# Routing a second mixture of experts: gate products in banks of their own, gathered rows' transposes spread between matmuls, and the first row list read between the halves of its weights

## The chip, the cores and the metric

The kernel runs on one core of a Trainium2 chip. The metric is the device time of one execution in microseconds (us); lower is better. A core has five engines with a queue each: TensorE (PE in the profile: matmuls and transposes; PEld is its weight load), VectorE (DVE), ScalarE (ACT), GpSimd (POOL: here small adds, and gathers and scatters by a list of rows), and SyncE (SP: here it only issues transfers). Each engine takes its instructions in the order of its queue and waits for the other engines by semaphores.

## The reference, cut to what matters

The program is an attention layer, then a mixture of eight experts in which each token goes through all of them, then a second mixture in which each token goes through two of eight experts only. The change touches the second mixture:

```python
logits = x @ w_gate                                   # x: 1152 x 512, 8 experts
noise_scale = np.log1p(np.exp(x @ w_noise))
noisy_logits = logits + noise_scale * noise
top2 = np.argpartition(-noisy_logits, 2, axis=1)[:, :2]
top2_l = np.take_along_axis(noisy_logits, top2, axis=1)
top2_w = softmax(top2_l)                              # shortened
for e in range(8):
    for k in range(2):
        mask = top2[:, k] == e
        h = np.maximum(x[mask] @ w1[e], 0.0)          # w1: 512 x 1024
        out[mask] += top2_w[mask, k, None] * (h @ w2[e])   # w2: 1024 x 512
```

## The kernel before, in words

**Tiles.** The 1152 tokens are nine tiles of 128. `acc` holds the output of the first mixture, nine tiles of 128 x 512. All products are of float32 operands split into a high and a low part (`xh`, `xl`; `wh`, `wl`; `hh`, `hl`), so one product is three matmuls (`mm3`, L161). ACT makes the high part and DVE the low one (`split`, L98), for weights too (`conv_w`, L113). PSUM has eight banks, in four tags "a" to "d" of two banks each (`ps`, L73); a new tile of a tag waits until the tile before the last one in it has been read.

**Order.** From L893 on the order on PE, DVE and ACT is the order of the code (`manual_schedule`, L893); POOL and SP, and after L987 all engines, are put in order by a scheduler that estimates times. `mm3` takes one step from the list `between` after each matmul, so small work can be laid between the large matmuls.

**Routing.** The last expert of the first mixture is worked off in two halves of its hidden size (`g1`, `g2` with `a0`, `b0`, `a1`, `b1`), and the routing of the second runs between, for three tiles at a time (`Route`, L367: `r0` for tiles 0 to 2, `r3`, `r6`). `turn` writes a tile of `acc` to the table of rows `x2d` in DRAM and transposes it (`x2t`, tag "b", then `xt` by ACT). The six steps of `steps` are three gate products (`lp`) and three sums (`lg`), with a DVE copy (`parts`) in the middle. `choose` and `weigh` (DVE, a little ACT) pick the two experts. `place` counts, on PE, how many tokens chose each expert before this one (`rank`), adds this block's choices to the running count `cnt` (three small adds on POOL, L462), computes each token's place and scatters (token, weight) to `table` in DRAM: six scatters on POOL (L474) per block. `total` (L524) is one matmul over `cnt`, run on PE once after `r3.place` (L935) and once in `rank` (L964).

**Experts of the second mixture.** Expert 0 starts with the rows that `r0` and `r3` placed: two row lists `tt` are read (L531), 2 x 128 rows gathered from `x2d` by POOL (`xg`, L536), transposed on PE (`xgt`, L722) and split, then `up` (first product, eight groups of hidden units) and `Down` (second product). Expert 0's rows out of `r6` are picked by matmuls with one-hot columns (`sort`, `assemble`: `hot`, `late`, L504). `rank` (L851) orders the other seven experts by their counts; SP loads that order into registers (L869), fetches the first one's weights (L965), and reads the seven row lists (`look`, L834). Then each expert is worked off by `expert`: first product, weights, gathers and transposes of the next one, second product, and a scatter with addition to `out` (`send`). Rows past 256 form a short `tail` of at most 64 rows (L802), whose second product is L809 and whose evacuation is L813.

Of the kernel before, what the change touches and what calls it, by code (L numbers as in the profile page):

```python
# [61 lines left out]
def tile_kernel(ctx: ExitStack, tc: tile.TileContext, qL, kL, vL, qS, kS, vS, wg, u12, w1, w2, wgn, noise, v1, v2, cst, dummy, out):  # L62
    nc = tc.nc
# [303 lines left out]
    class Route:  # L367
# [14 lines left out]
        def steps(self):  # L382
            def product(i):
                if i == 0:
                    self.lp = ps("b", "lp")
                for c in range(NC):
                    nc.tensor.matmul(self.lp[32 * c:32 * c + 32, i * 128:(i + 1) * 128], wgn_sb[:, c], self.xt[i][:, c],
                                     start=True, stop=True)
                if i == RB - 1:
                    self.parts = spool.tile([128, NC, 128], F32, tag="xt", name="parts", bufs=3)  # L390
                    nc.vector.tensor_copy(self.parts[:, :RB].rearrange("p c k -> p (c k)"), self.lp[:, :RB * 128])

            def total(i):
                if i == 0:
                    self.lg = ps("b", "lg2")
                nc.tensor.matmul(self.lg[:, i * 2 * E:(i + 1) * 2 * E], self.parts[:, i], fold2, start=True, stop=True)

            return [partial(product, i) for i in range(RB)] + [partial(total, i) for i in range(RB)]
# [315 lines left out]

    def prep_steps(xgs, ns, c0):
        n = sum(ns)

        def step(c):
            p = ps("b", "xgt")
            o = 0  # L720
# [52 lines left out]
    class Down:  # L773
# [28 lines left out]
        def tail(self, raws, hr, tt, k):  # L802
# [9 lines left out]
            for j in range(m):  # L812
                nc.scalar.activation(y[:k, j * d:(j + 1) * d], p[j * w:j * w + k, :d], AF.Copy,  # L813
                                     scale=tt[:k, 1:2].bitcast(F32))
            self.send(y, tt, k)
# [17 lines left out]

    def look():  # L834
        for i in range(E - 1):
            tt = cpool.tile([128, 3, 2], I32, name=f"tt{i}")
# [14 lines left out]
    def rank():  # L851
# [16 lines left out]
        nc.vector.tensor_copy(ordi, at)  # L868
        _, values = nc.values_load_multi_w_load_instructions(ordi[:1, :], engines=(mybir.EngineType.SP,), min_val=1, max_val=E - 1)  # L869
        order.extend(values)  # L870
        return past, key, spot

# [20 lines left out]
    with tc.manual_schedule(engines=ORDERED):  # L893
# [25 lines left out]
        r3.turn(0)  # L919
        g2(*b1, (5,), e, False)  # L920
        r0.choose()
        r3.turn(1)
        g1(*a0, whole[2:], 0, (0,))
        r0.weigh()
        r3.turn(2)
        spread(r3, 0, 2, 6, 9, 10, 11)
        r0.place(EARLY, float(LATE))
        g1(*a0, whole[2:], 0, (1,))
        r3.choose()
# [15 lines left out]
        g2(*b1, (6,), e, False)  # L945
        vs = [conv_w(raws[0])]
        g2(*b1, (7,), e, False)
        r6.turn(0)
        g2(*b1, (8,), e, False)
        r6.turn(1)  # L950
        prep([x for _, x in got], [128] * len(got), 0)
        r6.turn(2)
        spread(r6, 0, 1, 9, 18, 19, 20)
        up(ws, 0, 0, EARLY, (0,), "dac")
# [9 lines left out]
        ranked = rank()  # L964
        raws = [fetch_w(weights(v1, order[0], h)) for h in range(2)]  # L965
        look()
        r6.sort()
        up(ws, 0, 0, EARLY, (7,), "dac")
        got1 = fetch(0)
        d0 = Down(vs, [t for t, _ in got], [128] * len(got), 0)  # L970
        r6.assemble()
        d0.part(0, 0)
        d0.part(0, 1)
# [3 lines left out]
        rows = Rows(ws, EARLY, EARLY, LATE)  # L977
        rows.product(0)
        d0.part(1, 1)
        rows.turn(0)  # L980
        rows.product(1)
        ws = [conv_w(raws[0])]
        got = got1
# [5 lines left out]
    def expert(i, ws, got):  # L989
# [18 lines left out]
        d.part(0, 0)  # L1008
        d.part(1, 0)
        d.tail(raws, tail, tts[2], k)  # L1010
        d.part(0, 1)
# [104 lines left out]
```

## Time and profile before

| | us |
|---|---|
| median of 3 runs | 1129.99 (1126.79 to 1136.73) |
| the profiled execution | 1126.98 |
| its span, first to last instruction | 1125.0 |
| PE busy in the span | 1095.7 (97%) |
| DVE, ACT, POOL busy | 664.7, 393.7, 185.2 |

The profile is of one execution. Times in it are counted from the start of its span. PE is busy nearly all the time, so the places to read are the few gaps between its instructions: the time of the start of one instruction minus that of the one before it, against the same distance where nothing waits. What the gap waited for stands in brackets behind the instruction that ended it.

### The profile page before, as it was taken

The page shows a single profiled execution, that of the slowest core. Times are in us where ns is not written, and L with a number is a line of the kernel's source. Part 1 is how long each engine was busy: PE and PEld are TensorE (multiplying, and loading weights), DVE is VectorE, ACT ScalarE, POOL GpSimd, SP SyncE. Part 2 cuts the span into 40 slices and gives each one's busy share as a digit, 9 for nine tenths or more (in the row PEclk, how much of TensorE's full clock was granted, in tenths as well). Part 3 has the DMA queues.
Part 4 walks back from the last instruction along what each step waited for, and adds up shares of the span by engine and source line. Part 5 has one row for each costly group of instructions (what it writes and reads, how often), then busy time and mean ns, then how long its engine had stood idle before and what let it go on. Part 6 is the DMA issues. An engine that isn't in the chain of part 4 may idle for free.

```text
span 1125.0 us, 16986 instructions
## 1 busy us (share of the span) xinstructions
PE 1095.7 (97%) x6683; PEld 959.7 (85%) x6683; DVE 664.7 (59%) x1362; ACT 393.7 (35%) x884; POOL 185.2 (16%) x221
## 2 busy tenths in 40 slices
PE   7999999999999999999999999999998999999996
PEld 6787988999898998899988999899787788888885
DVE  5876795676666766666666666643356364544440
ACT  5631334333322333223332233221133263544441
POOL 3410132111111111211111110000041411222211
PEclk9999999999999999999999999999999999999998
DMA  9711152111111111111111111021122782555541
GB/s 304 217 52 73 38 174 86 38 63 50 38 39 38 55 59 38 38 38 51 64 38 39 38 46 68 4 109 38 57 48 76 175 318 27 195 194 194 171 100 23
DMA packets 31071, 98.71 MB, mean 88 GB/s; under 512 B 6506, under 2 KB 14954, under 8 KB 22412
## 3 DMA queue, kind: packets, MB, share of 16 engines
q1 hardware_dynamic: 16028, 80.52, 20.7%
q0 software_dynamic: 5200, 10.17, 4.5%
q10 hardware_dynamic: 9760, 6.89, 2.0%
q8 instruction: 54, 0.88, 0.3%
q14 instruction: 29, 0.24, 0.1%
HBM read 86.06 MB, written 11.60 MB: 87 GB/s over the span
## 4 chain that ended last, share of the span: by engine, by line
PE 88%; DVE 5%; DMA 3%; ACT 2%; issue 1%; SPq 0%; POOL 0%; POOLq 0%; DVEq 0%; ACTq 0%
PE y L163 42%; PE h L163 16%; PE a L637 13%; PE b L637 7%; PE d L637 3%; PE y L809 2%; DMA raw<-in_u 1%; PE xgt L722 1%; DMA qs<-in_qS 1%; DVE wl L105 1%; DMA wg_sb<-in_wg 1%; DVE u1l L105 1%; DVE acc L565 0%; PE ot L240 0%; ACT acc L610 0%
## 5 line engine op out<-in xcount | busy, mean ns | idle before, releaser
L561 DVE SCALAR_TENSOR_TENSOR acc<-y,P,acc 128x512 f32<-128x512 f32 x216 | 159.4, 748 | 147.0 <-PE y L163 147.0
L163 PE MATMUL y<-u2h,gh 128*128 128x512 f32 x504 | 198.5, 394 | 0.4 <-DVE acc L561 0.4
L163 PE MATMUL y<-u2l,gh 128*128 128x512 f32 x504 | 197.5, 392 | 0.0
L163 PE MATMUL y<-u2h,gl 128*128 128x512 f32 x504 | 189.8, 392 | 0.4 <-DVE gl L101 0.3
L153 POOL TENSOR_TENSOR ut<-raw 128x256 f32<-128x256 f32 x48 | 35.0, 751 | 509.8 <-DVE u1l L105 430.0
L163 PEld LDWEIGHTS y<-u2h,gl 128*128 128x128 f32 x504 | 94.4, 188 | 20.9 <-DVE gl L101 1.7
L163 PE MATMUL h<-xl,wh 128*128 128x384 f32 (+8 forms) x352 | 110.8, 315 | 0.0
L163 PE MATMUL h<-xh,wh 128*128 128x384 f32 (+8 forms) x352 | 109.9, 315 | 0.6 <-ACT xh L103 0.3
L163 PE MATMUL h<-xh,wl 128*128 128x384 f32 (+8 forms) x352 | 110.1, 313 | 0.0
L163 PEld LDWEIGHTS y<-u2h,gh 128*128 128x128 f32 x504 | 94.8, 188 | 15.8 <-issue 0.8
L163 PEld LDWEIGHTS y<-u2l,gh 128*128 128x128 f32 x504 | 94.8, 188 | 14.2
L100 ACT ACTIVATE hh<-h 128x256 fp32r<-128x256 f32 (+2 forms) x88 | 35.8, 415 | 99.8 <-PE h L163 96.0
L163 PEld LDWEIGHTS h<-xh,wh 128*128 128x128 f32 x352 | 66.5, 190 | 2.0 <-DVE hl L101 0.6
L163 PEld LDWEIGHTS h<-xl,wh 128*128 128x128 f32 x352 | 66.6, 189 | 1.5 <-issue 1.0
L103 ACT ACTIVATE u2h<-raw 128x1024 fp32r<-128x1024 f32 x31 | 32.9, 1061 | 98.9 <-PE y L163 98.9
L163 PEld LDWEIGHTS h<-xh,wl 128*128 128x128 f32 x352 | 66.6, 189 | 0.3 <-issue 0.2
L101 DVE SCALAR_TENSOR_TENSOR hl<-h,hh 128x256 fp32r<-128x256 f32 (+2 forms) x88 | 40.5, 464 | 38.8 <-ACT hh L100 37.0
L637 PE MATMUL a<-sh,u1h 128*128 128x288 f32 x192 | 57.4, 299 | 2.7 <-ACT s L643 2.7
L105 DVE TENSOR_TENSOR wl<-raw,wh 128x1024 fp32r<-128x1024 f32 x42 | 49.5, 1221 | 17.6 <-ACT wh L103 17.6
L637 PE MATMUL a<-sh,u1l 128*128 128x288 f32 x192 | 57.3, 298 | 0.0
L637 PE MATMUL a<-sl,u1h 128*128 128x288 f32 x192 | 57.1, 298 | 0.0
L637 PE MATMUL b<-sh,u1h 128*128 128x288 f32 x192 | 56.7, 295 | 0.0
(245 smaller groups left out, 2497.7 us busy)
## 6 DMA issues: line engine op xcount, KB each, us to landing
raw<-in_u SPq DMA_DIRECT2D x31, 1024.0 KB, 4.7
raw<-in_v SPq DMA_DIRECT2D x20, 1024.0 KB, 8.9
acc<-in_v SPq DMA_DIRECT2D x12, 1024.0 KB
raw<-in_w SPq DMA_DIRECT2D x4, 1024.0 KB
out<-zero ACTq DMA_DIRECT2D x1, 3072.0 KB
x2d<-acc ACTq DMA_DIRECT2D x9, 256.0 KB, 2.0
vs<-in_vL SPq DMA_DIRECT2D x4, 432.0 KB, 10.1
acc<-in_qL SPq DMA_DIRECT2D x3, 576.0 KB
```

Of the source, the lines that this page charges most:

```text
L100: seen[0] = nc.scalar.activation(hi, src, AF.Relu)
L101: nc.vector.scalar_tensor_tensor(lo, src, 0.0, hi.bitcast(F32), op0=ALU.max, op1=ALU.subtract)
L103: seen[0] = nc.scalar.activation(hi, src, AF.Copy)
L105: nc.vector.tensor_tensor(lo, src, hi.bitcast(F32), op=ALU.subtract)
L153: nc.gpsimd.tensor_tensor(t[:, o], x, y, op=ALU.subtract)
L163: nc.tensor.matmul(o, a, b, start=start, stop=stop)
L561: nc.vector.scalar_tensor_tensor(acc[:, t], p, P[:, t, scale:scale + 1], acc[:, t], op0=ALU.mult, op1=ALU.add)
L637: nc.tensor.matmul(p, l[:, b, c], m, start=first and i == 0, stop=i == 5, skip_group_check=not first)
L722: nc.tensor.transpose(p[:, o:o + k], xg[:k, c * 128:(c + 1) * 128], ident[:k, :k])
L809: nc.tensor.matmul(p[j * w:j * w + k, :d], hr[:, f, :k], raws[f // 4][:, f % 4, j * d:(j + 1) * d], start=f == 0, stop=f == 7)
```

## The change

Five edits:

1. The gate products (`lp`) go to tag "a" and their sums (`lg2`) to tag "c"; both were in "b", where the transposes and `rank` are. The products of `r3` are laid into the second hidden group of `g1`, so `r0.place` comes after that group instead of before it, and `r3.turn(1)` comes before `r0.choose`.
2. The transposes of expert 0's gathered rows go to tag "d" and are laid between the matmuls of the last `g2` tile, with `r6.turn(1)` among them; `r6.turn(2)` goes between the matmuls of `up`. The conversion of the first half of expert 0's second weights (`vs`) moves behind that `g2` tile.
3. The order of experts is loaded by SP in two parts: first one register, then the first half of that expert's weights, the first row list, the second half, then the other registers and lists.
4. The first quarter of expert 0's second product runs before the one-hot matmuls (`late`) instead of under them; the first half of the next expert's weights is converted one step earlier.
5. A tail's evacuation is shared by ACT and DVE, and in the last expert the tail's product runs last.

How instructions move. **POOL**, around the routing blocks `r0` and `r3` (`cnt` is the running count, `table` the DRAM table that is scattered to, `xg` the gather of rows for expert 0):

```order
 L462 TENSOR_TENSOR cnt<-cnt,m 128x8 x3
 L474 DMA table<-en,si 10240x2 x6
-L462 TENSOR_TENSOR cnt<-cnt,m 128x8 x3
+L462 TENSOR_TENSOR cnt<-cnt,m 128x8
 L474 DMA table<-en,si 10240x2 x6
+L462 TENSOR_TENSOR cnt<-cnt,m 128x8 x2
 L536 DMA xg<-x2d,tt 128x512 x2
```

The first two rows are `r0`'s adds and scatters, the next are `r3`'s. Before, the three adds of `r3` stood ahead of its six scatters; now one does, and two stand behind them.

**PE**, at the count `rank` of `r0`. Before (`x2t` is the transpose of tile 5, `h` the second hidden group, `lp` the first gate product of `r3`):

```order
L377 MATMUL x2t<-cs,acc 128x128 x4
L449 LDWEIGHTS upper
L449 MATMUL rank<-m,upper 128x24
L451 LDWEIGHTS onesb
L451 MATMUL rank<-m,onesb 128x16
L451 LDWEIGHTS onesb
L451 MATMUL rank<-m,onesb 128x8
L453 LDWEIGHTS onesb
L453 MATMUL rank<-cnt,onesb 128x24
L163 MATMUL h<-xh,wh 128x384
L387 MATMUL lp<-xt,wgn_sb 32x128 x4
```

and with the change (the last sum of `r3`, then `rank`, then the third hidden group):

```order
L163 MATMUL h<-xh,wl 128x384
L396 MATMUL lg_7631<-fold_97,parts 128x16
L449 LDWEIGHTS upper
L449 MATMUL rank<-m,upper 128x24
L451 LDWEIGHTS onesb
L451 MATMUL rank<-m,onesb 128x16
L451 LDWEIGHTS onesb
L451 MATMUL rank<-m,onesb 128x8
L453 LDWEIGHTS onesb
L453 MATMUL rank<-cnt,onesb 128x24
L163 MATMUL h<-xh,wh 128x384
```

`rank` of `r0` moved behind twelve large matmuls and the gate products and sums of `r3`. The two hidden groups that follow it, then `rank` of `r3`, two `g2` tiles and the matmul over `cnt` (L526) stand in the same order as before.

**SP**, from the load of the order of experts (`ordi`) to the first row list (L837, in the changed kernel L840; L875 is L869):

```order
-L869 TENSOR_LOAD ordi
-L869 ISA x14
-L110 ISA
-L110 DMA raw<-in_v 128x2048
+L110 DMA raw<-in_v 128x2048 x2
+L875 TENSOR_LOAD ordi
+L875 ISA x2
 L110 ISA
 L110 DMA raw<-in_v 128x2048
+L875 TENSOR_LOAD ordi
+L875 ISA x12
+L840 ISA
+L840 DMA tt_8199<-table 128x3x2
```

The first of two weight transfers now follows a load of one register, and the first row list comes ahead of the second weight transfer. (The line with `x2` holds transfers of expert 0's weights, both of which now follow the two row lists of L531; one of them stood ahead of these.)

The diff:

```diff
--- before.py
+++ after.py
@@ -382,7 +382,7 @@
         def steps(self):
             def product(i):
                 if i == 0:
-                    self.lp = ps("b", "lp")
+                    self.lp = ps("a", "lp")
                 for c in range(NC):
                     nc.tensor.matmul(self.lp[32 * c:32 * c + 32, i * 128:(i + 1) * 128], wgn_sb[:, c], self.xt[i][:, c],
                                      start=True, stop=True)
@@ -392,7 +392,7 @@
 
             def total(i):
                 if i == 0:
-                    self.lg = ps("b", "lg2")
+                    self.lg = ps("c", "lg2")
                 nc.tensor.matmul(self.lg[:, i * 2 * E:(i + 1) * 2 * E], self.parts[:, i], fold2, start=True, stop=True)
 
             return [partial(product, i) for i in range(RB)] + [partial(total, i) for i in range(RB)]
@@ -712,11 +712,11 @@
     hh = hpool.tile([128, 4, N], F32R, name="hh")
     hl = hpool.tile([128, 4, N], F32R, name="hl")
 
-    def prep_steps(xgs, ns, c0):
+    def prep_steps(xgs, ns, c0, bank="b"):
         n = sum(ns)
 
         def step(c):
-            p = ps("b", "xgt")
+            p = ps(bank, "xgt")
             o = 0
             for xg, k in zip(xgs, ns):
                 nc.tensor.transpose(p[:, o:o + k], xg[:k, c * 128:(c + 1) * 128], ident[:k, :k])
@@ -810,8 +810,11 @@
                                      start=f == 0, stop=f == 7)
             y = gpool.tile([128, DM], F32, tag="y", name="y", bufs=3)
             for j in range(m):
-                nc.scalar.activation(y[:k, j * d:(j + 1) * d], p[j * w:j * w + k, :d], AF.Copy,
-                                     scale=tt[:k, 1:2].bitcast(F32))
+                o, r, f = y[:k, j * d:(j + 1) * d], p[j * w:j * w + k, :d], tt[:k, 1:2].bitcast(F32)
+                if j % 2:
+                    nc.vector.tensor_scalar(o, r, f, None, op0=ALU.mult)
+                else:
+                    nc.scalar.activation(o, r, AF.Copy, scale=f)
             self.send(y, tt, k)
 
     def down(ws, tts, ns, o, last=False):
@@ -831,8 +834,8 @@
 
     lists = []
 
-    def look():
-        for i in range(E - 1):
+    def look(i, j):
+        for i in range(i, j):
             tt = cpool.tile([128, 3, 2], I32, name=f"tt{i}")
             nc.sync.dma_start(tt, table[ds(order[i] * ROWS, 384), :].rearrange("(t p) x -> p t x", p=128))
             lists.append(tt)
@@ -866,9 +869,11 @@
         nc.vector.tensor_tensor(big, spot, iota8[:, None, 1:].to_broadcast([128, n, n]), op=ALU.mult)
         nc.vector.tensor_reduce(at, big, axis=AX.X, op=ALU.add)
         nc.vector.tensor_copy(ordi, at)
-        _, values = nc.values_load_multi_w_load_instructions(ordi[:1, :], engines=(mybir.EngineType.SP,), min_val=1, max_val=E - 1)
+        return past, key, spot
+
+    def names(i, j):
+        _, values = nc.values_load_multi_w_load_instructions(ordi[:1, i:j], engines=(mybir.EngineType.SP,), min_val=1, max_val=E - 1)
         order.extend(values)
-        return past, key, spot
 
     def limits(past, key, spot):
         n = E - 1
@@ -918,14 +923,14 @@
         g2(*b1, (4,), e, False)
         r3.turn(0)
         g2(*b1, (5,), e, False)
+        r3.turn(1)
         r0.choose()
-        r3.turn(1)
         g1(*a0, whole[2:], 0, (0,))
+        r3.turn(2)
         r0.weigh()
-        r3.turn(2)
         spread(r3, 0, 2, 6, 9, 10, 11)
+        g1(*a0, whole[2:], 0, (1,))
         r0.place(EARLY, float(LATE))
-        g1(*a0, whole[2:], 0, (1,))
         r3.choose()
         g1(*a0, whole[2:], 0, (2, 3))
         r3.weigh()
@@ -943,14 +948,14 @@
         raws = [fetch_w(v2[0, h]) for h in range(2)]
         g1(*a1, whole[2:], 0, (1, 2, 3))
         g2(*b1, (6,), e, False)
-        vs = [conv_w(raws[0])]
         g2(*b1, (7,), e, False)
         r6.turn(0)
+        for k, step in enumerate(prep_steps([x for _, x in got], [128] * len(got), 0, "d")):
+            between.extend((None, partial(r6.turn, 1) if k == 1 else None, step))
         g2(*b1, (8,), e, False)
-        r6.turn(1)
-        prep([x for _, x in got], [128] * len(got), 0)
-        r6.turn(2)
-        spread(r6, 0, 1, 9, 18, 19, 20)
+        vs = [conv_w(raws[0])]
+        spread(r6, 0, 2, 11, 18, 19, 20)
+        between[5] = partial(r6.turn, 2)
         up(ws, 0, 0, EARLY, (0,), "dac")
         vs.append(conv_w(raws[1], True))
         up(ws, 0, 0, EARLY, (1,), "dac")
@@ -962,24 +967,28 @@
         r6.place(HEAD, over)
         up(ws, 0, 0, EARLY, (6,), "dac")
         ranked = rank()
-        raws = [fetch_w(weights(v1, order[0], h)) for h in range(2)]
-        look()
+        names(0, 1)
+        raws = [fetch_w(weights(v1, order[0], 0))]
+        look(0, 1)
+        raws.append(fetch_w(weights(v1, order[0], 1)))
+        names(1, E - 1)
+        look(1, E - 1)
         r6.sort()
         up(ws, 0, 0, EARLY, (7,), "dac")
         got1 = fetch(0)
         d0 = Down(vs, [t for t, _ in got], [128] * len(got), 0)
+        d0.part(0, 0)
         r6.assemble()
-        d0.part(0, 0)
         d0.part(0, 1)
         d0.part(1, 0)
         late = r6.collect(EARLY)
         limits(*ranked)
         rows = Rows(ws, EARLY, EARLY, LATE)
         rows.product(0)
+        ws = [conv_w(raws[0])]
         d0.part(1, 1)
         rows.turn(0)
         rows.product(1)
-        ws = [conv_w(raws[0])]
         got = got1
         prep([x for _, x in got], sizes(0), 384)
         rows.turn(1)
@@ -1007,6 +1016,11 @@
         d = Down(vs, tts[:2], (128, 128), 0)
         d.part(0, 0)
         d.part(1, 0)
+        if last:
+            d.part(0, 1)
+            d.part(1, 1)
+            d.tail(raws, tail, tts[2], k)
+            return ws, got
         d.tail(raws, tail, tts[2], k)
         d.part(0, 1)
         d.part(1, 1)
```

## Rows read from the trace of the kernel before

**Rows 1.** The page: span (head) and the chain that ended last (part 4).

```profile
span 1125.0 us, 16986 instructions
...
PE 88%; DVE 5%; DMA 3%; ACT 2%; issue 1%; SPq 0%; POOL 0%; POOLq 0%; DVEq 0%; ACTq 0%
```

**Rows 2.** Waits after 770 us: waiting engine, for whom: total us, times, longest.

```profile
PE xgt L722 <- DVE xl L105: 1.8, 3, 1.3
...
PE late L504 <- DVE hot L493: 1.6, 1, 1.6
...
PEld lp L387 <- DVE rk L455: 0.9, 1, 0.9
```

**Rows 3.** Timeline of PE, routing of r0 and r3: start us, us, instruction.

```profile
810.71 0.60 PE L377 MATMUL x2t<-cs,acc 128*128 128x128 f32 x4
811.98 0.17 PE L449 MATMUL rank<-m,upper 128*128 128x24 bf16 x1 [0.68 <-DVE m L431]
...
818.62 0.42 PE L163 MATMUL h<-xh,wh 128*128 128x384 f32 x1
...
828.68 0.18 PE L526 MATMUL cnt<-cnt,onesb 128*128 128x8 bf16 x1
```

**Rows 4.** Windows of PE: stretch, us, PE busy, granted clock, DMA share, GB/s.

```profile
814.00:814.50 0.50, 0.50 (x9) 0.57 0.00 0
...
817.00:817.50 0.50, 0.50 (x2) 0.52 0.00 0
...
1117.50:1118.00 0.50, 0.00 (x0) 0.85 0.46 74
...
1120.50:1121.00 0.50, 0.00 (x0) 0.50 0.23 37
```

**Rows 5.** Timeline of POOL, adds and scatters of r0 and r3.

```profile
812.31 0.76 POOL L462 TENSOR_TENSOR cnt<-cnt,m 128x8 bf16<-128x8 bf16 x3 [147.01 <-PE rank L453]
814.50 1.17 POOL L474 DMA_INDIRECT table<-en,si  x1 [1.43 <-DVE en L471]
...
821.05 0.96 POOL L474 DMA_INDIRECT table<-en,si  x1 [0.30 <-issue]
```

**Rows 6.** Timeline of PE, end of the first mixture and expert 0's transposes.

```profile
846.12 0.60 PE L377 MATMUL x2t<-cs,acc 128*128 128x128 f32 x4
...
846.79 0.39 PE L163 MATMUL y<-xwl,hh 128*128 128x512 f32 x1
847.02 0.40 PE L163 MATMUL y<-xwh,hl 128*128 128x512 f32 x1
...
849.78 0.38 PE L722 MATMUL xgt<-cs,xg 128*128 128x128 f32 x2
...
852.74 0.65 PE L377 MATMUL x2t<-cs,acc 128*128 128x128 f32 x4 [0.30 <-DVE xl L105]
```

**Rows 7.** Waits of SP's queue, 830 to 925 us.

```profile
SPq L837 <- DMA table<-en,si: 4.7, 1, 4.7
```

**Rows 8.** Timelines of POOL and SP, from r6's last scatter to the gather.

```profile
873.37 0.95 POOL L474 DMA_INDIRECT table<-en,si  x1 [0.31 <-issue]
883.88 0.98 POOL L536 DMA_INDIRECT xg<-x2d,tt  x1 [9.55 <-DMA tt<-table]
...
880.22 2.11 SPq L837 DMA_DIRECT2D tt<-table  x4
```

**Rows 9.** Timelines of DVE and PE, transposes of the next expert's rows.

```profile
890.39 2.35 DVE L105 TENSOR_TENSOR wl<-raw,wh 128x1024 fp32r<-128x1024 f32 x2
...
893.23 0.52 PE L722 MATMUL xgt<-cs,xg 128*128 128x128 f32 x3 [1.33 <-DVE xl L105]
```

**Rows 10.** Timelines of PE, ACT and POOL at the end.

```profile
1107.64 1.95 PE L809 MATMUL y<-acc,tail 128*32 128x128 f32 x64
...
1115.48 0.69 ACT L791 ACTIVATE y<-y,tt 128x512 f32<-128x512 f32 x1 [2.11 <-PEq L1021]
1116.44 1.56 POOL L795 DMA_INDIRECT out<-y,tt  x1 [1.24 <-ACT y L791]
```

## The prediction

> **What bounds the kernel now.** I read the page first: the chain that ended last is 88% PE over a span of 1125.0 us [rows 1]. So an edit is worth what it takes from PE's own time or from the gaps between PE's instructions, and work on DVE, ACT, POOL or SP costs nothing until PE waits for it. The list of waits after 770 us names the gaps in the part that is changed [rows 2]: each is short, at most 1.6 us, and each has an instruction of DVE behind it. Then I read PE's timeline around these gaps [rows 3, 6, 9, 10], the granted clock there [rows 4], and, because two of the moved steps issue transfers, the queues of POOL and SP [rows 5, 7, 8].
>
> **Edit 1: routing of r0 and r3.** Before, PE goes from the transpose of tile 5 at 810.71 to the third hidden group at 818.62, 7.91 us [rows 3]. In it lie a wait of 0.68 for `m` ahead of `rank` [rows 3], one of 0.9 for `rk`, because `lp` takes the bank of `rank` [rows 2], and a stretch at half clock: granted 0.57 in the half microsecond from 814.0 and 0.52 in that from 817.0, so it fell from 2.4 to 1.2 GHz at about 814.2 and rose again near 817.5 [rows 4]. 3.3 us at half speed do the work of 1.65. With own banks and `rank` behind the products both waits go, and without them I expect no fall of the clock: 7.91 - 0.68 - 0.9 - 1.65 = 4.7, plus 0.4 (my estimate from the distance of `lp` to `lg`) that `lg` now waits for DVE's copy, is 5.1. `rank` of r0 is done at 815.8, not 812.1, and the third group starts then, 2.8 us early.
>
> This gain doesn't reach the end, because of **POOL**. The matmul over `cnt` (828.68, [rows 3]) needs all three adds of r3. In the changed order two of them stand behind r3's six scatters, and all of r3's work on POOL stands behind r0's six. Before, r0's first scatter went out 2.5 us after `rank` (811.98 to 814.50), and the sixth started at 821.05 and took 0.96: 7.5 us for six [rows 3, 5]. Now:
> - r0's `rank` at 815.8; its DVE chain has one `hl` ahead of it and takes 2.6: first scatter at 818.4, sixth done at 825.9.
> - one add of r3 (three took 0.76 [rows 5], so 0.25): 826.2.
> - six scatters of r3 at the same 7.5, whose inputs DVE has ready by about 824.5, plus 0.3 ahead of them: 834.0.
> - two adds, 0.5, and their gap, 0.3: 834.8; with the signal PE runs the matmul at 835.1.
>
> PE gets there at 815.8 + (828.68 - 818.62 = 10.06) = 825.9, plus about 1.1 for which r3's `rank` now waits on DVE's longer queue: 827. So PE stands still for some 8 us, in one piece, and the matmul comes **6.4 us later** than before. Queued behind it on PE is everything else; on DVE the limit of r6 and the weight splits stand behind it too. Bounds from the scatters: 6 x 0.96 (no time between them) to 6 x 1.48 (the first to 1.17 plus 0.31) give 5.8 to 8.9 for six, two blocks of them -3.4 to +2.8 us; all twelve at either end is unlikely, so I keep +-1.
>
> The Trainium skill speaks against this size. Its page "DMA: Bandwidth & Descriptors", section "Anatomy of one DMA — SWDGE (gpsimd) path", puts the sequencer's dispatch of a DMA from GpSimd at about 50 ns and calls descriptor generation small, with most of the 2 us in the completion. By that, an estimate of six issues is 0.3 us and the adds would not be late, and the sum would be that of the first rival below. The trace doesn't agree: POOL's own row shows 0.96 per scatter and 1.3 from start to start.
>
> **The clock after it.** At the end of the kernel ACT takes PE's last result at 1115.48 [rows 10], and the clock granted is 0.85 in the half microsecond from 1117.5 [rows 4]: it fell some 2.4 us after PE's last work. The drop at 814 lasted 3.3 us with PE working [rows 4]. After 8 us of standing still PE starts at 1.2 GHz: **+1.65**, bounds 0 (it is up at once) and 3.3 (twice as long).
>
> **SP in this stretch.** The third weight transfer now stands behind the two row lists, which wait for r3's scatters. It goes out when its buffer is free, after the matmul and a weight split (2.35, as in [rows 9]), near 838, also past the lists; its first reader is now ACT behind the last `g2` tile, some 15 us later (849.78 [rows 6] and the shift): 0.
>
> **Edit 2: spread transposes.** From 849.78 to 852.74 PE does four pairs of transposes, 2.96 us [rows 6]. Laid between matmuls, a group of four costs 846.79 - 846.12 - 0.23 = 0.44 [rows 6]; a pair costs between half of that and all of it, four pairs 0.9 to 1.8. I take 1.05 (two of the four transposes at some 0.18, and 0.08 for starting again). Tag "d" has two banks, so the third and fourth pair and the first group of `up` wait for DVE's split two steps back; pairs are about 1 us apart, which covers it but for 0.2. `xt` of r6's last tile now waits behind a weight conversion on ACT, and covers itself within eleven matmuls. **-1.7**, bounds -0.9 and -2.1.
>
> **Edit 4: the one-hot matmuls.** The wait of 1.6 for `hot` [rows 2] is covered by twelve matmuls of 0.23 that go first. The picked rows come out later, but their split stands behind the same evacuation on ACT as before. **-1.6**, bounds -1.4 and -1.8.
>
> **Edits 3 and 4: next expert's rows.** Before, `wl` (2.35) stands on DVE right ahead of the splits of the transposed rows, and PE waits 1.33 for the first of them [rows 9]. With the weights' first half fetched some 2 us earlier and converted one step earlier, `wl` is out of the way and the splits can start up to 2.35 sooner. That needs the gather early as well, since PE is there 1.6 sooner: the list went out at 880.22 after a wait of 4.7 for r6's scatters, 5.9 after the last one (873.37 + 0.95) while two weight transfers ran, and the gather started at 883.88 [rows 7, 8]. Now only one transfer runs beside the scatters; I expect the list 2 to 3 us earlier. **-2.0** (2.35 less 0.3 of the transposes' own chain), bounds -0.7 (half of the 1.33) and -2.4. The second half of the weights goes out later; its first reader is the fifth of eight hidden groups, each of twelve matmuls, and it has some 10 us in hand.
>
> **Edit 5.** In the middle tails PE is the bound and ACT's half moves to idle DVE: 0. POOL now sends one output scatter before the gather of the expert after: its rows are used 20 us later, 0. At the end, ACT's evacuation of 128 x 512 took 0.69, the last scatter of 128 rows started at 1116.44 and its bytes moved until about 1120.8 [rows 4, 10]. Now PE ends with the tail (1.95 long either way), two pieces on each of ACT and DVE take about as long as that 0.69, and the last scatter moves 32 rows, behind the 128 that left 2 us before. **-1.0**, bounds -0.3 and -1.5.
>
> **Sum.** +6.4 + 1.65 - 1.7 - 1.6 - 2.0 - 1.0 = +1.75 us. Against the profiled execution that is 1126.98 + 1.75 = 1128.7. The median of the three runs is 3.0 above that execution, so for a median it is 1131.7; I say 1131.
>
> **Rivals.** A change under 1% (11 us) cannot be told from none here.
> - *The adds don't hold PE* (chance 0.10): POOL is free of a scatter sooner than its rows say, or the estimate of r0's chain is far off. Then the matmul over `cnt` comes at 827, -1.7, with no drop of the clock; with the other terms -8.0: 1119 against the profile, 1122 as a median. The gapless row of POOL speaks against it [rows 5].
> - *Slower: the gather stays where it was* (0.19). The list waits for scatters, not for weights, and goes out no earlier than 880 in the old count. PE, sooner by 1.6, then waits for the rows: both the 1.6 and the 2.0 are lost, +5.4, 1132.4 or 1135.4 as a median. It decides when the list goes out later than about 878.5. For it speaks the wait on the scatters [rows 7], against it that they waited beside 2 MB of weights.
> - *The spread doesn't do what it says* (0.05): pairs wait for DVE's splits as before (1.8 in three waits [rows 2]); the 1.7 shrinks to 0.5, +3, 1133 as a median.
>
> My forecast has the rest, 0.66. Its terms' bounds allow about -2 to +6 around the profile, 1128 to 1136 as a median, and runs spread by some 3 us below and 6 above their median. 1124 to 1137 holds all cases but the first rival and the ends. Faster by over 1% needs the first rival and every gain at its upper bound, 0.03; slower by over 1% needs the second with a clock that stays low and longer scatters, 0.05; within 1%: 0.92.
>
> **What would show it.** Right: a single gap on PE before the matmul over `cnt`, of 6 to 10 us, released by POOL's adds behind twelve scatters in one row, and half clock after it; no gap over 0.5 at `xgt` or `late`; `wl` ahead of `hl<-ht` on DVE; the gather 2 us or more earlier relative to r6's last scatter; about 4 us or less from the last scatter's start to its last byte. Wrong: PE reaches that matmul with POOL's adds done, or a gap in the gather's place.

## The result, and the profile after

The changed kernel is **slower** by 0.9%: median 1143.3 us (1132.6 to 1150.1, 20 runs) against 1133.3 us (1126.8 to 1138.9, 20 runs), a ratio of 1.0086 with a 95% interval of [1.0061, 1.0111]. The forecast was 1131, between 1124 and 1137. The profiled execution of the changed kernel took 1138.73 us, 11.75 more than that of before. Of the 12.3 us between forecast and median, 3.3 are no part of the change: the forecast was counted from a median of 1130.0 in three runs of the kernel before, and twenty gave 1133.3.

A number in brackets names the group of rows of the kernel before that is the same view. The page of the changed kernel, head and chain that ended last [rows 1]:

```profile
span 1136.6 us, 16988 instructions
...
PE 86%; DMA 5%; DVE 4%; POOL 2%; ACT 1%; issue 1%; SPq 0%; POOLq 0%; ACTq 0%; DVEq 0%
```

PE still bounds it, but DMA and POOL are now in the chain. The waits of PE after 770 us [rows 2], in the same columns:

```profile
PE cnt L526 <- POOL cnt L462: 7.3, 1, 7.3
PE xgt L722 <- DMA xg<-x2d,tt: 2.7, 3, 1.1
```

The three waits of before are gone; two others, longer, stand in their place.

Part of the 11.6 us of span has nothing to do with the change: the start differs from execution to execution, though in its first 40 us PE does the same instructions in the same order. The last matmul over `u2` (the end of the part that no edit touches) came between 738.4 and 750.9 us in the fourteen profiled executions of this study, at 739.15 before and at 742.77 with the change. In five of them, of the runs 3, 5, 6, 9 and 12 below, it came at 747.3 or later. There PE's instructions take longer until 38 us or later; the same group of twelve matmuls before and in run 3:

```profile
18.43 0.57 PE L240 MATMUL ot<-at,vs 96*64 96x64 f32 x12
```

```profile
20.75 0.91 PE L240 MATMUL ot<-at,vs 96*64 96x64 f32 x12
```

The profile's clock reads 1.00 in both places, so what makes the difference stays open. Below, every time is counted from that matmul over `u2`, and a step is the distance from one mark on PE to the next.

| mark on PE | before | changed | step | forecast of the step |
|---|---|---|---|---|
| transpose of tile 5 | 71.56 | 71.57 | 0 | 0 |
| third hidden group | 79.47 | 76.68 | -2.8 | -2.8 |
| matmul over `cnt` | 89.53 | 95.01 | +8.27, with the row above +5.48 | +6.4 in all |
| transpose of tile 6 | 106.97 | 114.14 | +1.69 | +1.65 |
| last `lg` of r6 | 118.68 | 124.04 | -1.81 | -1.7 |
| first `ht` | 147.21 | 150.75 | -1.82 | -1.6 |
| transposes of the expert after the next | 175.64 | 182.92 | **+3.74** | **-2.0** |
| end of the span | 385.85 | 393.83 | **+0.70** | **-1.0** |

The sum is +7.98 us instead of +1.75.

**The stall.** PE's timeline over the routing of r0 and r3 [rows 3]:

```profile
814.34 0.60 PE L377 MATMUL x2t<-cs,acc 128*128 128x128 f32 x4
...
819.35 0.17 PE L449 MATMUL rank<-m,upper 128*128 128x24 bf16 x1
...
819.45 0.42 PE L163 MATMUL h<-xh,wh 128*128 128x384 f32 x1
...
824.57 0.19 PE L449 MATMUL rank<-m,upper 128*128 128x24 bf16 x1 [0.71 <-DVE m L431]
...
837.78 0.17 PE L526 MATMUL cnt<-cnt,onesb 128*128 128x8 bf16 x1 [7.26 <-POOL cnt L462]
```

and POOL's beside it [rows 5]: r0's first and sixth scatter, one add of r3, r3's sixth scatter, the two other adds.

```profile
822.03 1.16 POOL L474 DMA_INDIRECT table<-en,si  x1 [1.59 <-DVE d L413]
...
828.57 0.96 POOL L474 DMA_INDIRECT table<-en,si  x1 [0.30 <-issue]
829.56 0.20 POOL L462 TENSOR_TENSOR cnt<-cnt,m 128x8 bf16<-128x8 bf16 x1
...
836.26 0.96 POOL L474 DMA_INDIRECT table<-en,si  x1 [0.30 <-issue]
837.25 0.48 POOL L462 TENSOR_TENSOR cnt<-cnt,m 128x8 bf16<-128x8 bf16 x2
```

PE waits 7.26 us in one piece, and the adds end at 837.73, 0.05 before it goes on. Windows of PE around it (stretch, us, PE busy, granted clock, DMA share, GB/s) [rows 4]:

```profile
831.00:834.00 3.00, 0.00 (x0) 1.00 0.02 1
834.00:836.00 2.00, 0.00 (x0) 0.70 0.03 1
836.00:838.00 2.00, 0.22 (x2) 0.50 0.03 1
838.00:840.00 2.00, 2.00 (x5) 0.50 0.00 0
...
841.00:842.00 1.00, 1.00 (x5) 0.68 0.92 107
```

The clock falls to 1.2 GHz while PE stands still and is up again between 841 and 842: some 3.9 us of work at half speed.

**The next expert's rows.** POOL: r6's last scatter and the first gather [rows 8].

```profile
882.09 0.96 POOL L474 DMA_INDIRECT table<-en,si  x1 [0.30 <-issue]
893.15 0.99 POOL L536 DMA_INDIRECT xg<-x2d,tt  x1 [10.10 <-DMA tt<-table]
```

SP: first half of the weights, the row list, second half [rows 8].

```profile
878.35 0.36 SPq L110 DMA_DIRECT2D raw<-in_v  x1
889.26 0.41 SPq L840 DMA_DIRECT2D tt<-table  x1
889.93 1.77 SPq L110 DMA_DIRECT2D raw<-in_v  x1
```

What SP's queue waits for ahead of the list is the scatters [rows 7]:

```profile
SPq L840 <- DMA table<-en,si: 7.5, 1, 7.5
```

The list goes out 6.2 us after the last scatter (882.09 + 0.96); it was 5.9 before. The gather starts 10.1 us after that scatter, 9.6 before. PE then waits for the rows themselves [rows 9]:

```profile
898.06 0.30 PE L722 MATMUL xgt<-cs,xg 128*128 128x128 f32 x1 [1.14 <-DMA xg<-x2d,tt]
898.90 0.33 PE L722 MATMUL xgt<-cs,xg 128*128 128x128 f32 x1 [0.54 <-DMA xg<-x2d,tt]
900.23 0.98 PE L722 MATMUL xgt<-cs,xg 88*128 88x88 f32 x4 [1.00 <-DMA xg<-x2d,tt]
```

and the clock falls again (a window of PE):

```profile
900.00:906.00 6.00, 5.77 (x23) 0.50 0.99 277
```

**The end** [rows 10], timelines of ACT, DVE and POOL:

```profile
1126.21 0.36 ACT L817 ACTIVATE y<-y,tt 32x128 f32<-32x128 f32 x1 [1.23 <-PE y L809]
1126.60 0.34 DVE L815 TENSOR_SCALAR y<-y,tt 32x128 f32<-32x128 f32 x1 [12.62 <-ACT y L817]
1126.98 0.36 ACT L817 ACTIVATE y<-y,tt 32x128 f32<-32x128 f32 x1 [0.41 <-DVE y L815]
1127.37 0.35 DVE L815 TENSOR_SCALAR y<-y,tt 32x128 f32<-32x128 f32 x1 [0.43 <-ACT y L817]
1128.00 1.34 POOL L795 DMA_INDIRECT out<-y,tt  x1 [1.19 <-DVE y L815]
```

The four pieces run one after another, each waiting for the other engine's, 1.51 us in all; before, the last piece was a single one of 0.69 [rows 10]. From the last scatter's start to the end of the span it is 8.6 us, as before (1125.0 - 1116.44), though it moves 32 rows and not 128. Nearly all of its bytes are through sooner: the DMA share falls to 0.04 at 1130.5, 2.5 us after its start, where before it took over 4.

### The profile page after: what moved, and what is told of

Read it like the earlier page. It is cut to its first block, busy times and chain, and to the rows that moved or that the text cites. A ratio compares the mean times of both kernels' runs of the same rounds, so it can differ in the third digit from the quotient of the medians.

```text
span 1136.6 us, 16988 instructions
## 1 busy us (share of the span) xinstructions
PE 1101.2 (97%) x6683; PEld 965.5 (85%) x6683; DVE 668.7 (59%) x1369; ACT 390.6 (34%) x877; POOL 183.3 (16%) x221
## 4 chain that ended last, share of the span: by engine, by line
PE 86%; DMA 5%; DVE 4%; POOL 2%; ACT 1%; issue 1%; SPq 0%; POOLq 0%; ACTq 0%; DVEq 0%
PE y L163 41%; PE h L163 16%; PE a L637 13%; PE b L637 7%; PE d L637 3%; PE y L809 2%; DMA raw<-in_u 2%; PE xgt L722 1%; POOL table L474 1%; DMA qs<-in_qS 1%; DMA wg_sb<-in_wg 1%; DVE u1l L105 1%; DMA table<-en,si 1%; DVE wl L105 1%; DVE acc L565 0%
```

## The experiments

My theory after the result: POOL's adds, then weights in flight beside the small transfers (scatters, list, gather), then the serial tail. For each run stand the ratio to the kernel before, and its marks, counted as above. The intervals of most of these ratios overlap, so the readings rest on the marks, which are of one profiled execution each. The code shows the lines that matter; `...` stands for lines left out.

**1. Adds first.**

```diff
-                    st = nc.gpsimd.indirect_dma_start(
+                    with tc.issue_after(last_add.ins):
+                        st = nc.gpsimd.indirect_dma_start(
                         ...
```

> The changed kernel with one thing different: POOL does all three adds of r3 to the running count before r3's six scatters. Theory A (the order on POOL holds PE): r0's sixth scatter is done at 829.5 as in the profile of the changed kernel, three adds of 0.25 follow, the count stands at 830.3 and PE, which is there at 830.5, waits under 0.5 instead of 7.26; the clock stays at full, which gives another 1.7; r3's scatters end some 0.7 later, and the gathered rows of expert 0 are then needed some 9 us earlier and come about when PE gets to them (wait 0 to 1). Together 8 to 9 us less than the changed kernel from the transpose of tile 6 on: ratio to the kernel before 1.000 to 1.002 instead of 1.009. Rival B (the adds are only the last of several releasers: PE is held by r0's scatters or by r3's choice of experts on DVE): a wait of 5 us or more is left before the same matmul, and the ratio stays at 1.007 or above. Rival C (the wait moves): PE stands as long at the transposes of expert 0's gathered rows, whose scatters end no earlier; ratio 1.005 or above, with a wait of 3 us or more there.

1.0040 [0.9992, 1.0088]. The stall is gone: the matmul over `cnt` comes at 87.61 with no wait. But rival C's wait is there as well, if shorter than the stall was; the waits of PE:

```profile
PE xgt L723 <- DMA xg<-x2d,tt: 5.2, 4, 2.7
```

3.9 us of these are at expert 0's rows. The edit was not clean here: the scheduler had also put the third weight transfer back ahead of the two row lists. The lists went out 4.2 us after the last scatter (2.2 in the changed kernel), the gather 4.6 after them (2.6): 4.0 later in all, as much as the wait. End of the span at 386.5: 7.3 us better than the change.

**2. The list behind both weight halves**, as before the change.

```diff
-        raws = [fetch_w(weights(v1, order[0], 0))]
-        look(0, 1)
-        raws.append(fetch_w(weights(v1, order[0], 1)))
+        raws = [fetch_w(weights(v1, order[0], h)) for h in range(2)]
+        look(0, E - 1)
```

> The changed kernel with the row list of expert 1 read behind both halves of its first weights, as before the change; the rest stays. Theory A (the list waits for the scatters whatever stands before it, and the second weight half, which now runs beside the list and the gather, slows both): the list still goes out about 6 us after r6's last scatter, but the rows of the three gathers land sooner after their issue; PE's three waits for gathered rows, 2.7 us together in the profile of the changed kernel, fall to under 1, the clock does not fall, and the rest of the kernel comes 3.5 to 4.5 us earlier: ratio 1.005 to 1.006 to the kernel before. Rival B (PE is merely there earlier; the weights' traffic does not matter): waits of 2 us or more stay, with the half clock after them, and the ratio stays within 0.001 of 1.009. Rival C (reading the list early was worth something): the list goes out 1 us or more later and the waits grow; 1.010 or above.

1.0113 [1.0026, 1.0201] from four runs, end at 397.9, rival C. The list goes out 7.7 us after the last scatter, and the waits are longer (POOL also sends an output scatter ahead of the gather here):

```profile
PE xgt L722 <- DMA xg<-x2d,tt: 7.2, 3, 4.2
```

So edit 3 was worth 4 us in these two executions, once edit 4 had brought PE there sooner. My theory had the second half as the culprit; both halves early are worse.

**3. The old end.**

```diff
-        if last:
-            d.part(0, 1)
-            ...
-                if j % 2:
-                    nc.vector.tensor_scalar(o, r, f, None, op0=ALU.mult)
```

> The changed kernel with its end undone: in the last expert the tail's product runs before the second halves, and the evacuation of the tails is all on ACT. Theory A (what counts is when the last scatter starts, not how many rows it moves: 8.6 us from its start to the end of the span in both profiles, 128 rows before and 32 after; and ACT and DVE take the tail's four pieces one after the other): from PE's last matmul to the last scatter's start 1.0 us instead of 1.9, the same 8.6 behind it, so 0.9 us less than the changed kernel, 1.0078 to the kernel before, and no wait of PE in the middle tails. Rival B (a scatter of fewer rows ends sooner): from the start of the last scatter to the end of the span it is 1 us or more longer than with 32 rows, and the time is not lower than that of the changed kernel. Either is below what the median can show; the rows of the profile decide.

1.0056 [1.0021, 1.0090]. From PE's end to the end of the span 9.6 us, as before, against 10.5 with the change. The last scatter (128 rows again) starts 8.55 before the end of the span, at 1142.8:

```profile
1134.25 1.55 POOL L795 DMA_INDIRECT out<-y,tt  x1 [1.25 <-ACT y L791]
```

Theory A. ACT alone takes 1.48 us for the tail's four pieces, so sharing them had saved nothing. PE doesn't wait in the middle tails.

**4. The rows' transposes inside the second product.**

```diff
-        prep([x for _, x in got], sizes(0), 384)
         rows.turn(1)
-        ws.append(conv_w(raws[1]))
+        for k, step in enumerate(prep_steps([x for _, x in got], sizes(0), 384)):
+            between.extend([None] * (2 if k else 11) + [step])
         down(vs, [late], [LATE], EARLY)
+        ws.append(conv_w(raws[1]))
```

> The changed kernel, but the transposes of expert 1's gathered rows no longer stand between the two halves of the rows of r6: they are laid between the matmuls of the last second product of expert 0, the first behind its twelfth matmul, and the conversion of the second half of the weights comes behind them. Theory A (PE's loss after the first mixture's end is the wait for the gathered rows and the half clock that follows it): PE reaches the transposes some 3 to 4 us later with work in between, waits under 0.5 us there, the clock stays at full, and the rest of the kernel comes 5 to 6 us earlier than in the changed kernel: ratio 1.0035 to 1.0045 to the kernel before. Rival B (the rows are late by more than that, or the wait moves to the splits on ACT and DVE or to the weights' second half): PE waits 2 us or more at the transposes or at the first hidden groups of expert 1, and the ratio stays at 1.007 or above.

1.0029 [0.9987, 1.0071], end at 388.5, 5.4 better than the change, no wait at the transposes. The clock reads 1.00 from 886 to 910 us. Theory A: PE's wait for these rows and the clock behind it are 5.4 of the 5.7 us by which the step missed its forecast. (The spread itself saves next to nothing: run 8 takes as long from the matmul over `cnt` behind r6 to the end as run 7, without it.)

**5. Adds first, third weight transfer behind the lists.** One `issue_after` more, around `fetch_w(v2[0, h])`.

> The changed kernel with r3's adds ahead of its scatters, as in the first run of this study, and with the third weight transfer kept behind the two row lists, where the changed kernel has it (in that run it had slipped ahead of them). Times from here on are counted from the last matmul over `u2` on PE to the end of the span, which leaves out the loads at the start, whose length differs from run to run by up to 10 us: 385.9 before, 393.8 in the changed kernel, 386.5 in that run. Theory A (a megabyte of weights in flight beside the scatters holds back their completion, the list and the gather; that, not the adds, made the wait of 3.9 us for expert 0's rows there): the lists go out about 2.2 us after r3's last scatter instead of 4.2, the gather 2.6 after them instead of 4.6, PE waits under 0.8 us for these rows, the clock stays up, and the time is 384 to 386, less than in that run by the 3.9 and up to 2 us of half clock, but with the waits for expert 1's rows back at 2 to 3 us and their half clock. Rival B (the scatters are late whatever runs beside them): the lists go out 4 us after the last scatter and PE's wait of 3 to 4 us stays.

1.0052 [1.0013, 1.0090], end at 392.6. Neither: the lists do go out 1.7 us after the last scatter and the gather 3.3 after them, but now two weight transfers run beside the gather, which takes 8.2 us to landing, and PE waits 3.3 + 1.0 us for expert 0's rows, and 4.7 more for expert 1's. What was held back moved one transfer on.

**6. Expert 1's list ahead of both weight halves**, nothing else moved.

```diff
-        raws = [fetch_w(weights(v1, order[0], 0))]
         look(0, 1)
-        raws.append(fetch_w(weights(v1, order[0], 1)))
+        with tc.issue_after(read[-1].ins):
+            raws = [fetch_w(weights(v1, order[0], h)) for h in range(2)]
```

> The changed kernel with the row list of expert 1 ahead of both halves of its first weights on SP; nothing else moves on any engine. Theory A (weights in flight hold back the scatters' completion): the list goes out 2 to 3 us after r6's last scatter instead of 6.2, the gather 2.6 to 4 us after it, the rows are there before PE is, no wait over 0.3 and no half clock at the transposes of expert 1; ACT may start the conversion of the first half 1 to 2 us later. From the last matmul over `u2` to the end 387.5 to 389 us instead of 393.8; ratio to the kernel before 1.003 to 1.005. Rival B (the scatters of r6 are late by themselves, six of them behind the output's traffic): the list goes out 5 us or more after the last scatter as before, and behind it the weights are 6 us later too, so that PE waits for the first half's conversion: 395 or more. Rival C (the gather is held back by the weights that now run beside it): the list is early, but PE still waits 2 us or more.

1.0038 [1.0002, 1.0073], end at 390.9. The list goes out 1.6 us after the last scatter instead of 6.2:

```profile
887.73 0.96 POOL L474 DMA_INDIRECT table<-en,si  x1 [0.30 <-issue]
```

```profile
890.33 0.42 SPq L840 DMA_DIRECT2D tt<-table  x1
```

The DMA issues between 872 and 893 us (line, queue, operation, count, KB each, median us from issue to landing) say why. Changed kernel:

```profile
raw<-in_v SPq DMA_DIRECT2D x2, 1024.0 KB, 7.6
table<-en,si POOLq DMA_INDIRECT x6, 7.7
```

This run:

```profile
raw<-in_v SPq DMA_DIRECT2D x2, 1024.0 KB, 5.6
table<-en,si POOLq DMA_INDIRECT x6, 2.5
```

The same six scatters of 128 rows land in 7.7 us with one megabyte of weights among them, in 2.5 without. That half of theory A is shown. The other half isn't: the weights now run beside the gather, PE still waits for the third of them,

```profile
904.06 0.59 PE L722 MATMUL xgt<-cs,xg 88*128 88x88 f32 x4 [0.91 <-DMA xg<-x2d,tt]
```

and its clock falls again (0.50 between 906 and 908), so 2.9 us came back, where theory A had 4.8 to 6.3. Rival C's wait of 2 us or more isn't reached either: the two waits are 1.1 together.

**7 and 8. Runs 1, 3, 5 and 6 together; and with run 4.**

> The changed kernel with all three: r3's adds ahead of its scatters and the third weight transfer behind the row lists; expert 1's list ahead of its weights; the end as before the change. Theory A: the gains of spread transposes and covered one-hot matmuls come through: 393.8 less 8.9 for the adds, 5.9 for the list and 0.9 for the end is 378 from the last matmul over `u2` to the end of the span, against 385.9 before, ratio 0.992 to 0.994. Rival B (the mended places meet other waits, PE now being some 9 us earlier at r6): 382 or more.

> The kernel of the run before this one with the transposes of expert 1's rows also laid into the last second product of expert 0. Theory A: the rows are there in time anyway, so the spread is worth the transposes' own 1 to 1.5 us at most: 376.5 to 378 from the last matmul over `u2` to the end. Rival B (without the list's order being enough, the rows come late): it is faster than that run by 2 us or more, since its transposes stand 3 to 4 us later.

0.9979 [0.9942, 1.0017] and 0.9973 [0.9936, 1.0011], ends at 384.5 and 385.7: rival B in run 7, and in run 8 neither number. What is left is the gather of expert 0, with both its weight transfers right behind the lists (run 7, 825 to 850 us):

```profile
xg<-x2d,tt POOLq DMA_INDIRECT x2, 8.1
```

8.1 us to landing, against 3.9 in the changed kernel. There one of the two transfers also went out behind the lists, at 840.50 and 1.5 us ahead of the gather, and the other only at 848.62: one megabyte did not hold this gather back, two did. In run 7 PE waits 3.6 us and its clock falls.

**9 and 10. Expert 0's second weights behind its gathered rows, from ACT's queue; 10 with edit 1 undone.**

```diff
-        raws = [fetch_w(v2[0, h]) for h in range(2)]
+            if k == 0:
+                between.append(lambda: raws.extend(fetch_w(v2[0, h], eng=nc.scalar) for h in range(2)))
```

> The kernel of the run before this one (e8) with expert 0's second weights (two transfers of 1 MB) issued from ACT's queue behind the first split of expert 0's gathered rows, and converted one hidden group later each; r3's row lists and gathers then have no weights beside them. Theory A (weights in flight hold back the gather as they hold back the scatters: 8 us from the gather's issue to the first transpose in the two runs before, against 3.8 where the weights were through): PE waits under 0.5 us for expert 0's rows, no half clock there; the last sum of r6 comes 9.9 us after the transpose of tile 6 instead of 15.5 to 16.8, and from the last matmul over `u2` to the end it is 378.5 to 380.5 us against 385.9 before, ratio 0.993 to 0.996. Rival B (the gather takes 8 us by itself after two blocks of scatters): the wait of 2.6 to 3.7 us stays, 385 or more. Rival C (the weights now come late): ACT stands at their conversion and PE waits 1.5 us or more for a hidden group of expert 0; 382 or more.

> The kernel of e9 with edit 1 undone for r0 and r3: gate products and sums in the bank of the transposes, `rank` of r0 ahead of the second hidden group again. Theory A (edit 1 is worth its 2.8 us less the 0.7 that r3's `rank` waits, once POOL's adds and the weights are out of the way): the matmul over the count comes at 89.5 instead of 87.6 behind the last matmul over `u2`, everything behind it 1.5 to 2.5 us later than in e9. Rival B (POOL's chain from `rank` of r0 to expert 0's rows sets the pace, and edit 1 starts it 3.7 us later): no difference between the two, or this one is earlier at the last sum of r6.

0.9974 [0.9942, 1.0007] and 0.9999 [0.9964, 1.0034], ends at 384.7 and 384.4. In run 9, with no weights beside them, the gathers land in 3.8 us and the wait for them is 0.76, from 3.7: theory A for the gather, nearly. But my edit took a step of `between` for itself and put `parts` behind a weight conversion on DVE:

```profile
865.81 0.40 PE L396 MATMUL lg<-fold,parts 128*128 128x16 f32 x2 [2.79 <-DVE parts L391]
```

Run 10 comes to the matmul over `cnt` only 0.7 us after run 9 (88.30, 87.61) and is 0.3 earlier at the end: rival B there, on which run 12 throws a doubt.

**11 and 12. That slip taken out, with and without edit 1.**

```diff
-            between.extend((None, partial(r6.turn, 1) if k == 1 else None, step))
-            if k == 0:
-                between.append(lambda: ...)
+            get = (lambda: ...) if k == 1 else None
+            between.extend((get, partial(r6.turn, 1) if k == 1 else None, step))
```

> The kernel of e9 with one slip of its own taken out: its weight transfers had taken a step of the list that is worked off between matmuls, which moved r6's last gate product into the second hidden group and DVE's copy of it (`parts`) behind the weight conversion; PE waited 2.8 us for it and fell to half clock. Here the transfers stand in a free step. Theory A (what is left then is the change's own gains): no wait for `parts`, under 0.8 us for expert 0's rows; the last sum of r6 comes at 115 to 116 behind the last matmul over `u2` (118.7 before the change, 119.3 in e9), PE's end at 369.5 to 371, the end of the span at 379 to 381 against 385.9: ratio 0.993 to 0.996. Rival B (another wait takes the place): 383 or more.

> The same mend in the kernel of e10, where edit 1 is undone for r0 and r3. Theory A (POOL's chain from `rank` of r0 to expert 0's rows gives back what edit 1 gains, 0.7 us at the matmul over the count): PE does not wait for expert 0's rows, and the end is within 0.7 us of the run before this one, 379 to 381. Rival B (edit 1 is worth 2 us, as forecast without POOL's stall): 1.5 us or more later than the run before this one.

Run 11 **beats both kernels**: 1123.8 us, ratio 0.9931 [0.9900, 0.9961]; last `lg` of r6 at 115.25, PE's end at 370.5, end of the span at 380.1, each within its expectation. PE's waits after 770 us, all of them:

```profile
PE ht L769 <- DVE hr L760: 0.8, 1, 0.8
PE rank L449 <- DVE i L426: 0.7, 1, 0.7
PE cnt L527 <- POOL cnt L462: 0.4, 1, 0.4
PE h L163 <- DVE hl L101: 0.3, 1, 0.3
```

Run 12: 0.9949 [0.9914, 0.9984], end at 383.6, rival B, 3.4 us later than run 11; it is at the matmul over `cnt` already 3.6 late. Most of that is the clock; the last section has its rows. But this profiled execution is the longest of run 12's twelve, and the intervals of the two ratios overlap: that edit 1 is worth as much in most executions is not shown.

## Why the prediction was wrong

- **Edit 1 and the stall: right.** The gain of 2.8 us, the twelve scatters in one row and the single gap are as forecast; r3's wait for DVE is 0.71, for 1.1. Only the size: +5.5 for 6.4, since from the end of r3's first add to PE's matmul it took 8.0 us (829.76 to 837.78), not 8.9. In the 2.8 two errors cancel: the 0.9 for `rk` is a wait of the weight load (PEld), and the matmul itself waited 0.60 (last section). Run 1 shows the adds as the cause. What I had not looked at is that expert 0's gathered rows are at the end of the same chain on POOL. They were late in runs 1 and 5; whether they would be with no weight transfer moved is not shown.
- **The Trainium skill against POOL's row: the row.** By the prediction's estimate from the Trainium skill's "DMA: Bandwidth & Descriptors", section "Anatomy of one DMA — SWDGE (gpsimd) path", the adds would have been on time. POOL's rows show 0.96 a scatter, and the wait came.
- **The clock: right**, +1.69 for 1.65, though so close by luck: the fall that the term was taken from lasted 3.3 us, this one 3.9, and the one at the next expert's rows over 6.
- **Edit 2 and the covered one-hot matmuls: right**, -1.81 for -1.7 and -1.82 for -1.6.
- **Edits 3 and 4, the next expert's rows: the step that failed.** "Now only one transfer runs beside the scatters; I expect the list 2 to 3 us earlier." One megabyte, sent with the third scatter (878.35), held them as long as two had that were sent from the sixth on (873.31): 6.2 against 5.9 us to the list. Run 6 shows that none leaves 1.6. `wl` did leave DVE's way, but PE, 1.8 us sooner, met rows that were not there: -2.0 became +3.74, 5.7 of the 6.2 us by which the sum was off (the too large stall takes 0.9 off, the end adds 1.7). The three waits are 2.7 us of it and the half clock, 5.77 us of work at 0.50, some 2.9: a fall of the clock behind a gap here had no term in the sum. It is the mechanism of the second rival (0.19): in the old count its list goes out at 889.26 - 742.77 - (124.04 - 118.68) + 739.15 = 880.3, past its point of 878.5. Its 5.4 was the whole change, 3.6 more than the forecast, against 5.7: it too lacked the clock. Its reason, that weights don't matter, was wrong: the list waits for scatters, and the scatters for weights.
- **Edit 5: wrong sign**, +0.7 for -1.0. I took two engines to halve the evacuation, but the four pieces are one chain of 1.5 us that now stands last in place of one piece of 0.69, and I counted the bytes of the last scatter where its start counts (run 3).

The same page of the Trainium skill has in its section "Queues, rings and completion order" that a transfer's semaphore is raised only after every earlier write of that DMA engine, whatever the queue. The direction agrees, 7.7 us to landing with weights and 2.5 without; that this is the reason no run here shows. The Trainium skill's section on the anatomy, on the same page, has the fixed cost of about 2.0 us scale with nothing; the 2.5 is near it, the 7.7 is not.

## What to carry to other kernels

Before a large transfer is issued, ask which small ones (scatters, lists, gathers) are on a chain that ends in the critical engine, and send it behind the last of them: moving it from one of them to the next only moves the wait. When a stall is taken away, look at what is next on the same chain; here no mend alone came under the 385.9 us of the kernel before (386.5 at best), and all of them together, in run 11, came to 380.1. Price the fall of the clock behind every gap that a change can open, not only behind the one expected. Count a gain of a few microseconds per step on the critical engine's marks, since the start alone moved the total by up to 12 us.

## What the runs showed of the hardware that I had not expected

- The scatters stayed late after the weights were through. Windows of the changed kernel, where the list goes out at 889.26:

```profile
882.00:884.00 2.00, 2.00 (x16) 1.00 0.91 374
884.00:885.00 1.00, 1.00 (x9) 1.00 0.05 2
885.00:889.00 4.00, 4.00 (x20) 1.00 0.00 0
```

The DMA engines are idle for four microseconds, and the landing of the last scatters is still out. That weights among them cause it is shown (run 6), how is open.

- The fall of the clock in the routing of r0 is not decided by the code. Before, in run 10 and in run 12 PE does the same instructions there, with the same two waits for `m` and `rk` (0.68 and 0.60, 0.66 and 0.59, 0.67 and 0.60 us), one profiled execution each. The windows, before,

```profile
814.00:817.50 3.50, 3.50 (x23) 0.51 0.01 0
```

run 10,

```profile
815.00:818.50 3.50, 3.50 (x32) 1.00 0.05 5
```

and run 12:

```profile
825.00:826.00 1.00, 1.00 (x12) 0.78 0.00 0
826.00:829.00 3.00, 3.00 (x18) 0.50 0.08 6
```

With the clock up the matmul over `cnt` comes at 88.30, with it down at 89.53 and 91.18. So edit 1, which takes these two waits of r0 away (87.6 in the runs that have it and no stall), is worth 0.7 us at this matmul where the clock stays up and 1.9 to 3.6 where it doesn't.
